# Column widths of the token tiles: 512 and 384 for 448 and 448 in the last layer but one, and 384 first in the early tiles

## The chip, the cores and the metric

The kernel runs on one core of one Trainium2 chip. The metric is the device time of one execution in microseconds (us); lower is better. TensorE is called PE below, VectorE DVE, ScalarE ACT, GpSimd POOL, and SyncE, which issues the loads, SP.

## The reference

```python
def _attn_ref(q, k, v):                      # 2 batches, 12 heads, 448 tokens, head size 64
    scores = np.matmul(q, k.transpose(0, 1, 3, 2)) / np.sqrt(64)
    scores = np.where(causal_mask, -1e9, scores)
    attn = softmax(scores)
    return np.matmul(attn, v)

def _moe_ref(x, w_in, w_out, alpha):         # 896 tokens, 768 -> 2048 -> 768
    h = x @ w_in
    g = np.maximum(h, 0.0) + alpha * np.minimum(h, 0.0)
    return g @ w_out

def _moe2_ref(x, w1, w2, w3, w_out):         # 896 tokens, 768 -> 768 -> 768
    h = np.maximum(np.maximum(x @ w1, x @ w2), x @ w3)
    return h @ w_out

# out = _moe2_ref(_moe_ref(attention as 896 x 768, ...), ...)
```

So there are four products by weight matrices after the attention: w_in (layer 1), w_out (layer 2), the three of w1, w2, w3 with a maximum over them (layer 3, the last but one), and the last w_out (layer 4).

## The kernel before, in words

**Precision.** Weights and activations are float32 values, each split into a high and a low part of the type fp32r. A product of two split values takes three matmuls (`product`, called on line 459): high by high, high by low, low by high. A weight matrix arrives as 64-bit words. The class `Weights` loads 128 output columns of it, converts the words on ACT (lines 422, 440) and DVE (lines 426, 429, 443, 454) and splits the result into `wh` (ACT, line 314) and `wl` (DVE, line 326). Four pairs `wh`, `wl` exist (ring `w`); the conversion runs ahead of PE by as many as are free.

**Tokens.** The activations lie transposed: 128 features in the partitions, the 896 tokens (2 batches of 448) in the free dimension. A PSUM bank holds 512 float32 columns, so the 896 tokens take two tiles, each with its own bank. Layers 1 and 2 use 512 and 384 columns (`CUT`, tokens 0 to 511 and 512 to 895, in layer 1; `LATE`, tokens 0 to 383 and 384 to 895, in layer 2). Layer 3 uses 448 and 448 (`HALF`). Layer 4 uses 448 columns throughout, because it computes its result by a scheme with seven products in place of eight over halves of the tokens and of the features; only its very last product is cut into 256 and 192 columns.

**Early tiles.** The first three blocks of 128 outputs of layer 1 (f = 0, 1, 2) begin while the last heads of the attention still run. Their first token tile is `SEQ[0]`, the 448 tokens of batch 0, in pieces of three matmuls (one of six feature blocks each) that are put into gaps of PE; their second tile is `SEQ[1]`, the 448 tokens of batch 1, after the attention. Each is followed by `prelu` on DVE and ACT. The slot of `w` that such a weight pair holds comes free with its second tile.

**Layer 3.** For each of six blocks f of 128 outputs, and each of w1, w2, w3, two products are made, one for each token tile, in an order that goes to and fro (`to_and_fro`: 1, 0, 0, 1, 1, 0, ...). One product is 6 feature blocks by 3 matmuls, 18 matmuls. The first result of a tile is copied out of its bank (ACT or DVE); the second and third are combined with the copy by a maximum on DVE (`larger`, line 984). Then the maxima are split (`h1`, `h2`, lines 314 and 326) and block sums of them are made for layer 4 (`room["t"]`, line 953). In the first three blocks the tile of batch 0 takes a buffer of the ring `mx` (three buffers of 448 columns), and that of batch 1 lies in the block sum's own place:

```python
m["m"] = room["t"][2][:, f] if kept else room["mx"].tile([P, S], F32, ...)
```

**Layer 4.** A step `third` waits for all products of layer 3; after it the operands of layer 4 are written over the tile that layer 3 read (`right`, `left`: casts and subtractions on ACT and DVE), while PE begins with the operands that are there already.

**Order.** Every engine executes its instructions in program order. That order comes from a list scheduler in the kernel's own code (`Plan`): each step has a rank, its cost on each engine that may do it, the steps it follows and the buffers it takes and gives; the step that can start first goes next, and of those within 0.02 us the one of the lowest rank. The cost of one matmul of n columns was `n / 2400 + 0.0134` us.

Of the kernel before, what the change touches and what calls it, by code (L numbers as in the profile page):

```python
# [25 lines left out]
NB = 3  # L26
# [36 lines left out]

def on_pool(n, two=True):
    return {"POOL": 0.18 + n * 2.1e-3 if two else 0.24 + n * 0.833e-3}


def on_dma(kb):
# [130 lines left out]
def attention_moe_moe2_kernel(  # L199
# [261 lines left out]
    class Product:  # L461


        def __init__(self, rank, pieces, bank, token, ranks=None):

            ranks = ranks or [rank] * len(pieces)
            total = len(pieces)
            self.end = None
            for i, (count, n, terms, after, give) in enumerate(pieces):
                self.end = plan.add(  # L470
                    ranks[i],
                    {"PE": count * 3 * (n / 2400 + 0.0134)},
                    step(self.issue, terms, bank, i == 0, i == total - 1),
                    list(after) + ([self.end] if self.end else []),
                    take=(token,) if i == 0 else (),
                    give=give,
                )
                if i == 0:
                    self.took = self.end
# [260 lines left out]
            return xT[i][:, self.hp, S * self.b : S * self.b + S]  # L740


    SEQ = tuple(slice(S * u, S * u + S) for u in range(B))
    CUT = tuple(slice(t, min(t + BANK, NT)) for t in range(0, NT, BANK))

    def to_and_fro(i, cut):
# [88 lines left out]
    for f, w in enumerate(held):  # L835
        r = FILL_RANK + FILL_STEP * f
        pieces = [
            (
                1,
                S,  # L840
                terms(w, lambda: xT, i, SEQ[0]),
                w.ready + [jobs[i].done],
                (("w", w.took),) * (i == KC - 1 and f < NB - HELD),
            )
            for i in range(KC)
        ]
        prod = Product(r, pieces, bank, "b")
        prelu(r + RANK["prelu"], prod, SEQ[0], f, lambda: early_g, "b")

# [13 lines left out]
    )  # L865
    for f in [*range(NB - HELD, NB), *(f for f in order if not NB - HELD <= f < NB)]:
        w = held[f] if NB - HELD <= f < NB else Weights(rank, w_in, 0, KC, f)
        us = SEQ[1:] if f < NB else [t for _, t in to_and_fro(f, CUT)]
        for u in us:
            after = w.ready + [j.done for j in jobs]  # L870
            pieces = [
                (
                    KC,
                    size(u),
                    lambda w=w, u=u: [t for i in range(KC) for t in terms(w, lambda: xT, i, u)()],
                    after,
                    (("w", w.took),) * (u == us[-1]),
                )
            ]
            prod = Product(rank, pieces, bank, "b")  # L880
            prelu(rank, prod, u, f, lambda: room["late_g"], "b")
        rank += 1
# [7 lines left out]
                self.it = self.make()  # L890
            return self.it

    LATE = (slice(0, NT - BANK), slice(NT - BANK, NT))
    yT = Lazy(lambda: pair(act, "x", [P, KC, NT]))
    y_done = {}
    for e in range(KC):
        pieces = [[] for _ in range(B)]
        for k, (k0, KW) in enumerate(((0, 6), (6, 5), (11, 5))):
            w = Weights(rank, w_out, k0, KW, e)
            for u, t in enumerate(LATE):  # L900
                pieces[u].append(
                    (
                        KW,
                        size(t),
                        lambda w=w, t=t, k0=k0, KW=KW: [
                            ([p[:, i, :] for p in w.parts], [p[:, t] for p in g[k0 + i]])
                            for i in range(KW)
                        ],
                        w.ready + [d for i in range(KW) for d in g_done[k0 + i]],
                        (("w", w.took),) * (u == (B - 1 if (e + k) % 2 == 0 else 0)),  # L910
                    )
                )
        prods = []
        for u in range(B):
            ranks = [rank + 0.2 * k + 0.1 * (u if (e + k) % 2 == 0 else 1 - u) for k in range(3)]
            prods.append(Product(rank, pieces[u], bank, "b", ranks))
        for u, t in enumerate(LATE):
            N = size(t)
            src = lambda u=u, N=N, prods=prods: prods[u].ps[:, :N]
            dst = lambda i, e=e, t=t: yT()[i][:, e, t]  # L920
            h = plan.add(rank, on_act(N, psum=True), copy(lambda dst=dst: dst(0), src), (prods[u].end,))
            y_done[u, e] = plan.add(
                rank,
                on_dve(N, psum=True),
                sub(lambda dst=dst: dst(1), src, lambda dst=dst: dst(0)),
                (h,),
                give=(("b", prods[u].took),),
            )
# [7 lines left out]
    def after_prelu():  # L936
# [1 line left out]
        early.close()  # L938
        last = ctx.enter_context(tc.tile_pool(name="last", bufs=1))
        room["tk"] = last  # L940
        room["mx"] = ctx.enter_context(tc.tile_pool(name="mx", bufs=3))
        room["h1"] = pair(last, "h1", [P, KH, S])
        room["h2"] = pair(last, "h2", [P, KH, NT])
        room["w1"] = pair(last, "w1", [P, KG, EH * P])
        room["w2"] = pair(last, "w2", [P, KH, EH * P])
        room["t"] = [last.tile([P, KH, S], F32, tag=f"t{i}", name=f"t{i}") for i in range(3)]
        room["s"] = [last.tile([P, KH, EH * P], F32, tag=f"s{i}", name=f"s{i}") for i in range(3)]
        plan.buffers(at=plan.end[second], mx=3, tk=1)

    second = plan.add(0, {"NONE": 0.0}, step(after_prelu), list(y_done.values()))  # L950
    def plus(out, a, b, op=ALU.add):
# [8 lines left out]
    h_done, t_done, s_done, products, low_done = {}, {}, {}, [], {}  # L960
    for f in range(KG):
        ws = [Weights(rank, w, 0, KC, f) for w in (w1, w2, w3)]
        m, m_end = [{} for _ in range(B)], [None] * B
        for i in range(3):
            for u, cut in to_and_fro(KG + f + i + 1, HALF):
                pieces = [
                    (
                        KC,
                        S,
                        lambda w=ws[i], u=cut: [t for x in range(KC) for t in terms(w, yT, x, u)()],  # L970
                        ws[i].ready + [y_done[v, e] for v in ((0, 1), (1,))[u] for e in range(KC)],
                        (("w", ws[i].took),) * (u == (B - 1 if (KG + f + i) % 2 else 0)),
                    )
                ]
                prod = Product(rank, pieces, bank, "b")
                products.append(prod.end)
                kept = f < KH and u == 1

                def first(m=m[u], f=f, kept=kept):
                    m["m"] = room["t"][2][:, f] if kept else room["mx"].tile([P, S], F32, tag="m", name="m")  # L980
                    return m["m"]

                def larger(prod=prod, m=m[u]):
                    nc.vector.tensor_tensor(
                        out=m["m"], in0=prod.ps[:, :S], in1=m["m"], op=ALU.max
                    )

                if i == 0:
                    m_end[u] = m_took = plan.add(
                        rank,  # L990
                        on_act(S, psum=True) | on_dve(S, psum=True),
                        copy(first, lambda prod=prod: prod.ps[:, :S]),
                        (prod.end,),
                        take=() if kept else ("mx",),
                        give=(("b", prod.took),),
                    )
                    m[u]["took"] = m_took
                else:
                    m_end[u] = plan.add(
                        rank,  # L1000
                        on_dve(S, psum=True),
                        step(larger),
                        (prod.end, m_end[u]),
                        give=(("b", prod.took),),
                    )
        k = f % KH
        for u in range(B):
            if f < KH and u == 1:
                continue
            dst = lambda i, f=f, k=k, u=u: room["h1"][i][:, k] if f < KH else room["h2"][i][:, k, HALF[u]]  # L1010
            src = lambda m=m[u]: m["m"]
            h = plan.add(rank, on_act(S), copy(lambda dst=dst: dst(0), src), (m_end[u],))
            h_done[u, f] = plan.add(
                rank,
                on_dve(S),
                sub(lambda dst=dst: dst(1), src, lambda dst=dst: dst(0)),
                (h,),
                give=(("mx", m[u]["took"]),) if f >= KH and u == 0 else (),
            )
        t = lambda i, k=k: room["t"][i][:, k]  # L1020
        m0, m1 = (lambda m=m[u]: m["m"] for u in range(B))
        if f < KH:
            t_done[0, k] = plan.add(
                rank,
                on_dve(S),
                step(plus(partial(t, 0), partial(t, 2), m0, ALU.subtract)),
                (m_end[1], h_done[0, f]),
                give=(("mx", m[0]["took"]),),
            )
        else:  # L1030
            t_done[1, k] = plan.add(
                rank,
                on_dve(S),
                step(plus(partial(t, 1), m1, partial(t, 0), ALU.subtract)),
                (m_end[1], t_done[0, k]),
            )
            t_done[2, k] = plan.add(
                rank,
                on_dve(S),
                step(plus(partial(t, 2), m1, partial(t, 2), ALU.subtract)),  # L1040
                (t_done[1, k], h_done[1, f]),
                give=(("mx", m[1]["took"]),),
            )
        r = f // 2
        c = slice(r * P, r * P + P)
# [155 lines left out]
    class Bank:  # L1201
# [3 lines left out]
        def add(self, rank, w, x, w_after, x_after, give=(), after=(), parts=(slice(0, S),)):  # L1205
            ends = []
            for cols in parts:
# [1 line left out]
                first = self.took is None  # L1209
                end = plan.add(  # L1210
                    rank,
                    {"PE": KH * 3 * (n / 2400 + 0.0134)},
                    step(self.issue, w, x, first, cols),
                    [*chain, *w_after, *x_after, *after],
                    take=("b",) if first else (),
# [254 lines left out]
```

## Time and profile before

| | |
|---|---|
| median of 3 runs | 492.85 us (491.95 to 492.85) |
| the profiled execution | 492.2 us |
| its span, first to last instruction | 490.4 us |
| granted clock of TensorE | 1.00 of full speed |
| busy: PE, DVE, ACT, POOL | 483.9, 384.6, 251.1, 51.8 us |

The span is what the trace covers; 1.8 us of the profiled execution's time lie outside it. Matmuls are pipelined: the time from one matmul's start to the next one's start is what PE needs for it, and is shorter than the duration that a row gives for it.

### The profile page before, as it was taken

What the parts mean: (1) busy time and instruction counts of PE and PEld (TensorE: products, weight loads), DVE (VectorE), ACT (ScalarE), POOL (GpSimd) and SP (SyncE); (2) the same over time, 40 slices, a digit from 0 to 9 for tenths busy, and PEclk for the clock granted to TensorE, in tenths of its full rate; (3) what the DMA queues carried; (4) which work ended last, traced back from release to release, by engine and by line L of the source; (5) the groups of instructions that cost most, each with busy time, mean ns of one, the idle gap of its engine ahead of it and who ended that gap; (6) DMA issues with size and microseconds to landing.
All of it is one profiled execution on the core that took longest, in us unless ns stands there. A gap on an engine that the chain in (4) does not pass through costs nothing.

```text
span 490.4 us, 7332 instructions
## 1 busy us (share of the span) xinstructions
PE 483.9 (99%) x2727; PEld 420.0 (86%) x2727; DVE 384.6 (78%) x751; ACT 251.1 (51%) x478; POOL 51.8 (11%) x100
## 2 busy tenths in 40 slices
PE   8999999999999999999999999999999999999997
PEld 4766768999988899889989989999999999999886
DVE  5789997589999999855756657599899998716962
ACT  6899995254455455432524434454564744305510
POOL 5657664000000000000000000000000000000000
PEclk9999999999999999999999999999999999999999
DMA  8666512113323343333334234344353633000122
GB/s 293 228 214 212 178 41 78 52 65 128 128 77 124 124 120 115 111 118 119 106 93 145 63 110 144 112 155 169 128 193 117 205 129 130 0 1 1 57 95 75
DMA packets 13859, 58.28 MB, mean 119 GB/s; under 512 B 1664, under 2 KB 3328, under 8 KB 13824
## 3 DMA queue, kind: packets, MB, share of 16 engines
q1 hardware_dynamic: 13680, 57.72, 35.2%
q8 instruction: 21, 0.34, 0.3%
q14 instruction: 14, 0.11, 0.1%
q10 hardware_dynamic: 144, 0.10, 0.1%
HBM read 55.06 MB, written 2.75 MB: 118 GB/s over the span
## 4 chain that ended last, share of the span: by engine, by line
PE 91%; ACT 5%; DVE 2%; issue 1%; POOL 0%; DVEq 0%; ACTq 0%
PE ps L459 82%; ACT e L672 3%; PE ps L641 3%; PE pv L731 3%; PE pt L716 3%; DVE e L659 1%; ACT p L314 1%; PE warm L797 1%; PE pt L713 0%; ACT xh L314 0%; ACT wh L314 0%; POOL e L689 0%; DVE wl L326 0%; DVE sm L684 0%; ACT r L440 0%
## 5 line engine op out<-in xcount | busy, mean ns | idle before, releaser
L459 PE MATMUL ps<-xh,wh 128*128 128x448 f32 (+2 forms) x435 | 159.4, 366 | 0.0
L459 PE MATMUL ps<-xh,wl 128*128 128x448 f32 (+2 forms) x435 | 159.2, 366 | 0.0
L459 PE MATMUL ps<-xl,wh 128*128 128x448 f32 (+2 forms) x435 | 159.1, 366 | 0.0
L459 PEld LDWEIGHTS ps<-xl,wh 128*128 128x128 f32 x435 | 81.7, 188 | 8.3
L459 PEld LDWEIGHTS ps<-xh,wl 128*128 128x128 f32 x435 | 81.6, 188 | 8.3
L459 PEld LDWEIGHTS ps<-xh,wh 128*128 128x128 f32 x435 | 81.7, 188 | 8.2
L314 ACT CAST wh<-t 128x768 fp32r<-128x768 f32 (+1 forms) x52 | 42.2, 812 | 63.3 <-DVE t L454 62.4
L459 PE MATMUL ps<-g_h,wl 128*128 128x384 f32 (+1 forms) x192 | 69.7, 363 | 0.0
L459 PE MATMUL ps<-g_l,wh 128*128 128x384 f32 (+1 forms) x192 | 69.6, 363 | 0.0
L459 PE MATMUL ps<-g_h,wh 128*128 128x384 f32 (+1 forms) x192 | 69.5, 362 | 0.0
L326 DVE TENSOR_TENSOR wl<-t,wh 128x768 fp32r<-128x768 f32 (+1 forms) x49 | 45.2, 922 | 18.0 <-ACT wh L314 18.0
L422 ACT ACTIVATE t<-raw 128x768 f32<-128x768 f32 (+1 forms) x58 | 51.2, 886 | 8.9 <-DMA raw<-in_moe_w_out_dram 2.9
L454 DVE CUSTOM_DVE_ANT_0 t<-t,r 128x1536 uint16<-128x1536 uint16 (+1 forms) x58 | 53.4, 925 | 2.1
L443 DVE SCALAR_TENSOR_TENSOR t<-raw,t 128x768 uint32<-128x768 uint32 (+1 forms) x58 | 53.7, 925 | 0.9
L440 ACT ACTIVATE r<-raw 128x768 uint32<-128x768 uint32 (+1 forms) x58 | 51.1, 881 | 3.9 <-DMA raw<-in_moe_w_in_dram 2.0
L689 POOL TENSOR_SCALAR e<-e,sm 128x192 f32<-128x192 f32 (+3 forms) x84 | 43.7, 539 | 29.8 <-DVE sm L685 18.7
L672 ACT ACTIVATE e<-e,nm 128x192 f32<-128x192 f32 (+3 forms) x84 | 43.9, 529 | 5.1 <-DVE nm L659 5.0
L314 ACT CAST g_h<-g 128x384 fp32r<-128x384 f32 (+2 forms) x32 | 18.1, 567 | 47.1 <-DVE g L769 47.0
L459 PEld LDWEIGHTS ps<-g_l,wh 128*128 128x128 f32 x192 | 36.0, 188 | 4.0
L459 PEld LDWEIGHTS ps<-g_h,wh 128*128 128x128 f32 x192 | 36.1, 188 | 3.9
L459 PEld LDWEIGHTS ps<-g_h,wl 128*128 128x128 f32 x192 | 36.0, 188 | 3.8
L659 DVE CUSTOM_DVE_ANT_0 e<-ps,mask 128x192 f32<-128x192 f32 (+2 forms) x72 | 32.1, 486 | 8.2 <-PE ps L641 7.9
(95 smaller groups left out, 521.9 us busy)
## 6 DMA issues: line engine op xcount, KB each, us to landing
raw<-in_moe_w_dram SPq DMA_DIRECT2D x18, 768.0 KB, 4.3
raw<-in_moe_w_in_dram SPq DMA_DIRECT2D x16, 768.0 KB, 4.4
raw<-in_moe_w_out_dram SPq DMA_DIRECT2D x12, 768.0 KB, 4.3
raw<-in_moe_w_out_dram SPq DMA_DIRECT2D x12, 640.0 KB, 4.1
qk<-in_qk_dram SPq DMA_DIRECT2D x12, 448.0 KB, 3.4
v<-in_v_dram SPq DMA_DIRECT2D x12, 448.0 KB, 4.8
out_dram<-o SPq DMA_DIRECT2D x11, 224.0 KB, 1.9
out_dram<-o SPq DMA_DIRECT2D x1, 128.0 KB, 1.7
```

The lines of the kernel that those rows point to most:

```text
L314: nc.scalar.copy(out(), src())
L326: ENGINE[engine].tensor_tensor(out=out(), in0=a(), in1=f32(b()), op=ALU.subtract)
L422: nc.scalar.activation(out=f32(self.t), in_=f32(self.raw[..., 1]), func=AF.Abs)
L440: nc.scalar.activation(out=self.r, in_=self.raw[..., 0], func=AF.Copy, scale=2.0**-29)
L443: nc.vector.scalar_tensor_tensor(out=self.t, in0=self.raw[..., 1], scalar=0xC0000000, in1=self.t, op0=ALU.bitwise_and, op1=ALU.bitwise_or,)
L454: ENGINE[engine].tensor_tensor(out=t, in0=t, in1=self.r.bitcast(I32), op=ALU.add)
L459: nc.tensor.matmul(ps, a, c, start=(first and y == 0), stop=(last and y == 2), **kw)
L641: nc.tensor.matmul(ps if c else ps[rows * j : rows * j + rows], self.qk[d, 0, START[c] : START[c] + rows], self.qk[d, 1, S - n :] if j els ...
L659: nc.vector.tensor_tensor_reduce(out=self.e_part(c, j), in0=self.ps[c, j], in1=masks[j][:, m : m + n] if c else short, op0=ALU.add, op1=AL ...
L672: nc.scalar.activation(out=s, in_=s, func=AF.Exp, scale=-1.0, bias=self.column(self.nm, i, c, j), accum_out=self.column(self.sm, i, c, j),)
L689: ENGINE[engine].tensor_scalar(out=s, in0=s, scalar1=self.column(self.sm, i, c, j), scalar2=1.0, op0=ALU.mult, op1=ALU.mult,)
L716: nc.tensor.transpose(pt[:, o : o + P], self.e[:, s : s + P], ident)
```

## The change

The token tiles of layers 1, 2 and 3 now all use `CUT`, 512 and 384 columns. In layer 2 that exchanges the two tiles' places (before, the first one was the narrow one). In layer 3 the products, first copies and maxima have 512 and 384 columns in place of 448 and 448. Because layer 4 still wants halves of 448, the maxima of both tiles go into one tile of 896 columns (`m["m"]`), whose halves the splits and block sums read; a split or sum that needs tokens 448 to 895 now waits for both tiles' maxima. In the first three blocks that tile is `both`, which holds the block sums 0 and 2 later; sum 0 is made in place. In the last three blocks it is one of two buffers of the ring `mx`. The early tiles take tokens 0 to 383 first (`EARLY`), which need batch 0 alone as before, and tokens 384 to 895 after the attention. The planner's cost of a matmul whose width is no multiple of 128 is 0.0066 us higher than before (`moved`).

```diff
+def moved(n):
+    return n / 2400 + (0.02 if n % 128 else 0.0134)
...
-                    {"PE": count * 3 * (n / 2400 + 0.0134)},
+                    {"PE": count * 3 * moved(n)},
...
-    SEQ = tuple(slice(S * u, S * u + S) for u in range(B))
+    EARLY = slice(0, NT - BANK)
...
-                S,
-                terms(w, lambda: xT, i, SEQ[0]),
+                size(EARLY),
+                terms(w, lambda: xT, i, EARLY),
...
-        prelu(r + RANK["prelu"], prod, SEQ[0], f, lambda: early_g, "b")
+        prelu(r + RANK["prelu"], prod, EARLY, f, lambda: early_g, "b")
...
-        us = SEQ[1:] if f < NB else [t for _, t in to_and_fro(f, CUT)]
+        us = [slice(EARLY.stop, NT)] if f < NB else [t for _, t in to_and_fro(f, CUT)]
...
-    LATE = (slice(0, NT - BANK), slice(NT - BANK, NT))
...
-            for u, t in enumerate(LATE):
+            for u, t in enumerate(CUT):
...
-        room["mx"] = ctx.enter_context(tc.tile_pool(name="mx", bufs=3))
+        room["mx"] = ctx.enter_context(tc.tile_pool(name="mx", bufs=2))
...
-        room["t"] = [last.tile([P, KH, S], F32, tag=f"t{i}", name=f"t{i}") for i in range(3)]
+        both = last.tile([P, KH, NT], F32, tag="t0", name="t0")
+        room["m"] = both
+        room["t"] = [both[:, :, HALF[0]], last.tile([P, KH, S], F32, tag="t1", name="t1"), both[:, :, HALF[1]]]
...
-            for u, cut in to_and_fro(KG + f + i + 1, HALF):
+            for u, cut in to_and_fro(KG + f + i + 1, CUT):
+                N = size(cut)
...
-                        ws[i].ready + [y_done[v, e] for v in ((0, 1), (1,))[u] for e in range(KC)],
+                        ws[i].ready + [y_done[u, e] for e in range(KC)],
...
-                def first(m=m[u], f=f, kept=kept):
-                    m["m"] = room["t"][2][:, f] if kept else room["mx"].tile([P, S], F32, tag="m", name="m")
-                    return m["m"]
-
-                def larger(prod=prod, m=m[u]):
+                def first(m=m, f=f, cut=cut):
+                    if not m:
+                        m["m"] = room["m"][:, f] if f < KH else room["mx"].tile([P, NT], F32, tag="m", name="m")
+                    return m["m"][:, cut]
+
+                def larger(prod=prod, m=m, N=N, cut=cut):
                     nc.vector.tensor_tensor(
-                        out=m["m"], in0=prod.ps[:, :S], in1=m["m"], op=ALU.max
+                        out=m["m"][:, cut], in0=prod.ps[:, :N], in1=m["m"][:, cut], op=ALU.max
                     )
...
-                        on_dve(S, psum=True),
+                        on_dve(N, psum=True),
...
-            src = lambda m=m[u]: m["m"]
-            h = plan.add(rank, on_act(S), copy(lambda dst=dst: dst(0), src), (m_end[u],))
+            src = lambda m=m, u=u: m["m"][:, HALF[u]]
+            h = plan.add(
+                rank, on_act(S), copy(lambda dst=dst: dst(0), src), m_end if u else m_end[:1]
+            )
...
-                step(plus(partial(t, 0), partial(t, 2), m0, ALU.subtract)),
-                (m_end[1], h_done[0, f]),
-                give=(("mx", m[0]["took"]),),
+                step(plus(partial(t, 0), partial(t, 2), partial(t, 0), ALU.subtract)),
+                (*m_end, h_done[0, f]),
...
-                    {"PE": KH * 3 * (n / 2400 + 0.0134)},
+                    {"PE": KH * 3 * moved(n)},
```

## Rows read from the trace of the kernel before

**Rows 1.** The page: the span, and the busy time of each engine.

```profile
span 490.4 us, 7332 instructions
PE 483.9 (99%) x2727; PEld 420.0 (86%) x2727; DVE 384.6 (78%) x751; ACT 251.1 (51%) x478; POOL 51.8 (11%) x100
```

**Rows 2.** The chain that ended last: start us, us, what.

```profile
85.62 376.32 PE ps L459 x1850
...
465.40 0.62 DVE o L1362
...
466.16 20.91 PE ps L459 x108
```

**Rows 3.** Windows: us, busy PE, PEld, DVE, ACT, POOL, clock, DMA share, GB/s.

```profile
85.62:103.28 17.66, 17.66 (x87) 16.38 (x88) 11.46 (x19) 6.07 (x10) 0.00 (x0) 1.00 0.10 40
103.28:197.35 94.07, 94.07 (x469) 84.66 (x468) 93.04 (x148) 47.78 (x68) 0.00 (x0) 1.00 0.35 115
197.35:313.18 115.83, 115.83 (x578) 104.24 (x576) 73.63 (x104) 47.16 (x66) 0.00 (x0) 1.00 0.35 112
313.18:447.09 133.91, 133.91 (x649) 121.64 (x649) 107.40 (x158) 62.35 (x84) 0.00 (x0) 1.00 0.34 118
...
447.09:466.16 19.07, 18.76 (x92) 16.74 (x90) 18.48 (x36) 13.19 (x28) 0.00 (x0) 1.00 0.10 37
...
331.00:404.00 73.00, 73.00 (x355) 66.31 (x354) 68.12 (x102) 40.55 (x54) 0.00 (x0) 1.00 0.46 158
```

**Rows 4.** Timeline of PE: start us, duration us, then the instruction and its form.

```profile
75.28 0.45 PE L459 MATMUL ps<-xh,wh 128*128 128x448 f32 x1
...
92.34 0.37 PE L459 MATMUL ps<-xh,wh 128*128 128x448 f32 x1
...
103.28 0.33 PE L459 MATMUL ps<-xh,wh 128*128 128x384 f32 x1
...
106.43 0.39 PE L459 MATMUL ps<-xh,wh 128*128 128x512 f32 x1
...
110.55 0.39 PE L459 MATMUL ps<-xh,wh 128*128 128x512 f32 x1
...
114.63 0.33 PE L459 MATMUL ps<-xh,wh 128*128 128x384 f32 x1
...
120.90 0.39 PE L459 MATMUL ps<-xh,wh 128*128 128x512 f32 x1
...
310.55 0.33 PE L459 MATMUL ps<-g_h,wh 128*128 128x384 f32 x1
...
313.18 0.36 PE L459 MATMUL ps<-xh,wh 128*128 128x448 f32 x1
...
395.01 0.37 PE L459 MATMUL ps<-xh,wh 128*128 128x448 f32 x1
...
447.09 0.37 PE L459 MATMUL ps<-h1h,w1h 128*128 128x448 f32 x1
```

**Rows 5.** Line 459 on PE in layer 3: duration min/median/max, first and last start.

```profile
L459 PE MATMUL ps<-xh,wh x216: 362/368/368, 313.2 to 446.5; 128*128 128x448 f32 x108
```

**Rows 6.** Groups by line and form: busy us, mean ns, idle before.

```profile
L984 DVE TENSOR_TENSOR m<-ps,m 128x448 f32<-128x448 f32 x18 | 11.2, 624 | 17.6 <-PE ps L459 17.3
...
L326 DVE TENSOR_TENSOR xl<-ps,xh 128x512 fp32r<-128x512 f32 x6 | 4.2, 692 | 14.6 <-ACT xh L314 14.6
...
L326 DVE TENSOR_TENSOR xl<-ps,xh 128x384 fp32r<-128x384 f32 x6 | 3.3, 557 | 9.8 <-ACT xh L314 9.8
```

**Rows 7.** Timeline of DVE, at four places.

```profile
108.17 0.95 DVE L326 TENSOR_TENSOR wl<-t,wh 128x768 fp32r<-128x768 f32 x1
...
311.37 0.69 DVE L326 TENSOR_TENSOR xl<-ps,xh 128x512 fp32r<-128x512 f32 x1 [3.46 <-ACT xh L314]
...
389.54 1.95 DVE L326 TENSOR_TENSOR wl<-t,wh 128x768 fp32r<-128x768 f32 x2
...
447.29 0.62 DVE L984 TENSOR_TENSOR m<-ps,m 128x448 f32<-128x448 f32 x1 [1.84 <-PE ps L459]
```

More of the change, by code (lines that the diff above doesn't have):

```diff
@@ L916, in attention_moe_moe2_kernel @@
             prods.append(Product(rank, pieces[u], bank, "b", ranks))
-        for u, t in enumerate(LATE):
+        for u, t in enumerate(CUT):
             N = size(t)
@@ L945, in after_prelu @@
         room["w2"] = pair(last, "w2", [P, KH, EH * P])
-        room["t"] = [last.tile([P, KH, S], F32, tag=f"t{i}", name=f"t{i}") for i in range(3)]
+        both = last.tile([P, KH, NT], F32, tag="t0", name="t0")
+        room["m"] = both
+        room["t"] = [both[:, :, HALF[0]], last.tile([P, KH, S], F32, tag="t1", name="t1"), both[:, :, HALF[1]]]
         room["s"] = [last.tile([P, KH, EH * P], F32, tag=f"s{i}", name=f"s{i}") for i in range(3)]
-        plan.buffers(at=plan.end[second], mx=3, tk=1)
+        plan.buffers(at=plan.end[second], mx=2, tk=1)
     second = plan.add(0, {"NONE": 0.0}, step(after_prelu), list(y_done.values()))
@@ L962, in attention_moe_moe2_kernel @@
         ws = [Weights(rank, w, 0, KC, f) for w in (w1, w2, w3)]
-        m, m_end = [{} for _ in range(B)], [None] * B
+        m, m_end, took = {}, [None] * B, None
         for i in range(3):
-            for u, cut in to_and_fro(KG + f + i + 1, HALF):
+            for u, cut in to_and_fro(KG + f + i + 1, CUT):
+                N = size(cut)
                 pieces = [
@@ L968, in attention_moe_moe2_kernel @@
                         KC,
-                        S,
+                        N,
                         lambda w=ws[i], u=cut: [t for x in range(KC) for t in terms(w, yT, x, u)()],
-                        ws[i].ready + [y_done[v, e] for v in ((0, 1), (1,))[u] for e in range(KC)],
+                        ws[i].ready + [y_done[u, e] for e in range(KC)],
                         (("w", ws[i].took),) * (u == (B - 1 if (KG + f + i) % 2 else 0)),
@@ L976, in attention_moe_moe2_kernel @@
                 products.append(prod.end)
-                kept = f < KH and u == 1
-                def first(m=m[u], f=f, kept=kept):
-                    m["m"] = room["t"][2][:, f] if kept else room["mx"].tile([P, S], F32, tag="m", name="m")
-                    return m["m"]
-                def larger(prod=prod, m=m[u]):
+                def first(m=m, f=f, cut=cut):
[3 more added lines that the diff above has]
+                def larger(prod=prod, m=m, N=N, cut=cut):
                     nc.vector.tensor_tensor(
-                        out=m["m"], in0=prod.ps[:, :S], in1=m["m"], op=ALU.max
+                        out=m["m"][:, cut], in0=prod.ps[:, :N], in1=m["m"][:, cut], op=ALU.max
                     )
                 if i == 0:
-                    m_end[u] = m_took = plan.add(
+                    m_end[u] = plan.add(
                         rank,
[L991 to L994, printed above, removed]
+                        on_act(N, psum=True) | on_dve(N, psum=True),
+                        copy(first, lambda prod=prod, N=N: prod.ps[:, :N]),
+                        (prod.end,) + ((took,) if took else ()),
+                        take=("mx",) * (f >= KH and took is None),
                         give=(("b", prod.took),),
                     )
-                    m[u]["took"] = m_took
+                    took = took or m_end[u]
                 else:
@@ L1017, in attention_moe_moe2_kernel @@
                 (h,),
-                give=(("mx", m[u]["took"]),) if f >= KH and u == 0 else (),
             )
         t = lambda i, k=k: room["t"][i][:, k]
-        m0, m1 = (lambda m=m[u]: m["m"] for u in range(B))
+        m0, m1 = (lambda m=m, u=u: m["m"][:, HALF[u]] for u in range(B))
         if f < KH:
@@ L1034, in attention_moe_moe2_kernel @@
                 step(plus(partial(t, 1), m1, partial(t, 0), ALU.subtract)),
-                (m_end[1], t_done[0, k]),
+                (*m_end, t_done[0, k]),
             )
@@ L1040, in attention_moe_moe2_kernel @@
                 step(plus(partial(t, 2), m1, partial(t, 2), ALU.subtract)),
-                (t_done[1, k], h_done[1, f]),
-                give=(("mx", m[1]["took"]),),
+                (t_done[1, k], h_done[0, f], h_done[1, f]),
+                give=(("mx", took),),
             )
```

## The prediction, made before the change was run

> **What bounds the kernel now.** I read the page first: PE is busy 483.9 of a span of 490.4 us, DVE 384.6 [rows 1]. Busy shares alone don't make a bound, so the chain that ended last comes next. From 85.62 us on it is one piece of 376.32 us of line 459 [rows 2]: through layers 1, 2, 3 and the start of layer 4, PE waits for nothing that the trace shows. After that one wait of PE remains, at 466.16, for a DVE instruction that ran from 465.40 to 466.02 [rows 2]. The windows by stage say the same: PE is busy for the whole of each stretch from 85.62 to 447.09, at a granted clock of 1.00, the level of 2.4 GHz [rows 3]. So what counts is how long PE takes from one matmul's start to the next, and any microsecond saved there comes off the end, as long as weights and free banks still arrive in time.
>
> **The price of a width.** The timeline gives it where the width changes [rows 4]. From 106.43 to 114.63 there are 36 matmuls of 512 columns: 8.20 / 36 = 227.8 ns each. From 114.63 to 120.90 there are 36 of 384: 6.27 / 36 = 174.2 ns. A pair covers 896 columns in 14.47 / 36 = 401.9 ns. Whole layers agree: layer 1 from 103.28 to 197.35 is 234 pairs (13 blocks of 18; the window's count has one matmul of the neighbour), 94.07 / 234 = 402.0 ns, and layer 2, 288 pairs, 115.83 / 288 = 402.2 ns [rows 3]. In these numbers the cost of changing from one width to the other, if there is one, is contained, and at the same frequency as in the new layer 3, about once in 36 matmuls. Layer 3 takes 133.91 us [rows 3] for 6 x 3 x 2 x 18 = 648 matmuls of 448: 206.7 ns each, 413.3 ns for the 896 columns. The early tiles show a third value: from 92.34 to 103.28 there are 54 of 448 [rows 4], 202.6 ns each.
>
> The same columns and the same number of instructions therefore cost 11.4 ns less as 512 + 384 than as 448 + 448 in layer 3, and 3.3 ns less than in the early tiles. From 384 to 512 a column costs 53.6 / 128 = 0.42 ns; at that slope a matmul of 448 would take 201.0 ns, so 448 carries an excess of 5.7 ns in layer 3 and 1.6 ns early on.
>
> The Trainium skill's page "TensorE: Matmul & The Clock Gate" (section "Back-to-back issue gap") speaks against this change: warm, it puts the gap at N / 2.4 ns plus a fixed 2.5 ns whatever N is. By it two matmuls cost 378.3 ns for 896 columns however they are cut, and layer 3 would gain nothing. The trace does not agree: its gaps are 227.8, 206.7 and 174.2 ns, where the page gives 215.8, 189.2 and 162.5, and the one of 448 lies off the line of the other two. I go by the rows and keep the rule's outcome as a rival.
>
> **The change, part by part.**
>
> Layer 3: 648 matmuls of 448 become 324 pairs. 324 x 401.9 = 130.2 us against 133.91: **-3.7 us**. With layer 2's 402.2 it would be -3.6; these bounds are close because each is a mean over hundreds.
>
> Early tiles: 54 pairs at 401.9 in place of 2 x 202.6 = 405.2 ns: **-0.2 us** in total. The first halves start at 75.28 [rows 4]; 21 of their 54 matmuls run before 85.62, between the steps of the last heads. Those 21 now take 21 x 28.4 ns = 0.6 us less. If the planner puts another piece there (3 matmuls, 0.52 us) nothing is lost; if PE idles instead, 0.6 us is lost. Bounds -0.2 to +0.4; I take -0.2, since pieces are left to fill with. The weights of the next block are the tightest of layer 1: their `wl` ends at 109.12 [rows 7] and PE wants them at 110.55 [rows 4]. The lead of 1.4 us stays nearly the same, as PE's total up to there does.
>
> Layer 2: the same widths with places exchanged. 0.
>
> Order at the seam: layer 2 now ends with its tile of 512 and layer 3 starts with the 384 others, 18 x 174.2 ns = 3.1 us, before it reads the 512. How long such a tile takes to be ready: PE had ended one at 310.55 [rows 4] and its `xl` was done at 312.06 [rows 7], 1.5 us later. Hidden, with 1.6 us to spare.
>
> First copies and maxima: DVE takes 692 ns for 512 columns and 557 for 384 out of PSUM, 1249 together, against 2 x 624 = 1248 [rows 6]. 0. The splits and block sums keep their count and width. Waiting for both maxima delays a block's sums by at most one product, 18 x 0.23 = 4.1 us; behind them on DVE stand conversions, see below. Two `mx` buffers: a block's buffer is wanted again two blocks later, and a block lasts 133.91 / 6 = 22.3 us. 0.
>
> Layer 4: PE's work is unchanged. DVE is nearly full there (18.48 of 19.07 us [rows 3]) and begins with the last maximum at 447.29, just behind PE's end of layer 3 [rows 4, 7]; the operands it then writes lie over what layer 3 reads, so its work moves forward together with PE. The last maximum has 384 columns now: 0.07 us less, off PE's wait at 466.16. **-0.1 us**. The dearer 448 in the planner can exchange steps on DVE; an instruction of DVE more or less ahead of that wait is about 0.6 us [rows 6], so -0.5 (the wait is gone: PE's last matmul before it began at about 465.5) to +0.6, or twice that if it happens in two rounds.
>
> What covers all this is the conversion of weights on DVE: 68.12 of 73.00 us between 331 and 404 [rows 3]. The tightest pair is the twelfth of layer 3: the first of the two `wl` from 389.54 ends at about 390.5 [rows 7], PE begins on it at 395.01 [rows 4]. PE will be there 11 x 18 x 11.4 ns + 0.2 = 2.4 us earlier, so 2.1 of 4.5 us of lead remain if DVE does not get faster. No stall.
>
> Sum: 492.2 (the profiled execution's own time: span 490.4 and 1.8 around it) - 3.7 - 0.2 - 0.1 = 488.2 us. That execution is 0.65 us under the median of the runs, which lie from 491.95 to 492.85; for the time of a median I add about half of that: **488.6 us**.
>
> **The rivals.**
>
> (a) More than that, 0.10: the 448s of layer 4 run at the early 202.6 ns (180 of them, 0.7 us), or PE's wait there goes. 487.6. Against it: layer 3 began after a run of 384, too, and ran at 206.7 from start to end; the durations hardly vary [rows 5].
>
> (b) Part is given back, 0.10: DVE's order in layer 4 or an idle PE between the last heads costs 0.6 to 1.5 us. 489.8.
>
> (c) The excess belongs to the stage and not to the width. If only the part by which layer 3 exceeds the early tiles does (4.1 ns a matmul), a pair costs 410.1 there and 1.0 us is gained: about 491.3, chance 0.04. If all 5.7 ns do, a pair costs 413.3: no gain in layer 3, 492.3, chance 0.05. For it: the same width ran at two rates. Against it: 512 and 384 ran alike in layers 1 and 2 while DVE was busy 99% and 64%, and nothing in layer 3's steady durations looks like interference. The skill's rule above ends in the same place.
>
> (d) Slower, 0.05: the weights come late in layer 3. Maxima that now wait in DVE's queue for the wider product push conversions back. It begins to cost when DVE is over 2.1 us later at the twelfth pair than now, and makes the kernel slower beyond 2.1 + 4.0 = 6.1 us; DVE has 4.9 us of slack in that stretch. With 7 us, 493.5.
>
> **How the numbers follow.** The forecast, 488.6 with a range of its own from 487.9 to 489.3, has 0.66. A measurement of this kernel tells about 0.2%, 1 us, from no change. Faster by more: forecast, (a), (b) and the first half of (c), 0.90. Within: the second half of (c), 0.05. Slower: (d), 0.05. The range that holds 8 in 10 takes in (a) and (b) but neither (c) nor (d), and the unknown half microsecond between an execution and a median: 487.2 to 490.2.
>
> **What would show it.** In the trace after, layer 3's stretch should last about 130.2 us with 36 matmuls of 512 in 8.2 us and 36 of 384 in 6.3; PE should have no idle time from about 85 to layer 4; layer 4 should last what it does now, 43.3 us from the first `h1` matmul to the end of the span. The prediction is wrong if the gap of 512 or 384 in layer 3 is above that of layers 1 and 2, if PE waits for `wl` around layer 3's twelfth weights, or if PE's wait in layer 4 grows past 1 us.

## The result, and the profile after

The changed kernel takes 488.2 us in the median of four runs (487.7 to 488.75) against 492.55 for the kernel before: a ratio of 0.9914, with a 95% interval from 0.9896 to 0.9931. That is 4.35 us faster, 0.4 us below the forecast and inside its range. Measured a second time it took 488.34, a ratio of 0.9914 again [0.9899, 0.9928].

The page of the changed kernel, to be set beside [rows 1] (line 463 of it is line 459 of the kernel before, 318 is 314, 330 is 326, 990 is 984): the span is 3.8 us shorter, and PE's busy time falls by nearly as much, while DVE's hardly changes.

```profile
span 486.6 us, 7335 instructions
PE 480.6 (99%) x2727; PEld 415.6 (85%) x2727; DVE 384.0 (79%) x750; ACT 250.3 (51%) x478; POOL 53.7 (11%) x101
```

Windows of the changed kernel (columns as in [rows 3]): layer 1, layer 3, the stretch from 331 to 404, and layer 4 up to PE's one wait. PE is still busy without a break up to layer 4.

```profile
103.75:197.75 94.00, 94.00 (x469) 84.63 (x468) 93.48 (x147) 46.93 (x67) 1.84 (x1) 1.00 0.34 115
313.62:443.84 130.22, 130.22 (x649) 117.23 (x648) 105.70 (x157) 62.68 (x84) 0.00 (x0) 1.00 0.36 122
331.00:404.00 73.00, 73.00 (x365) 65.72 (x364) 69.34 (x106) 40.91 (x55) 0.00 (x0) 1.00 0.46 161
443.84:462.74 18.90, 18.76 (x91) 16.74 (x91) 18.70 (x37) 13.55 (x29) 0.00 (x0) 1.00 0.10 37
```

Layer 3 takes 130.22 us where it took 133.91. The timeline of PE shows it run by run, to be read as [rows 4]: 36 matmuls of 512 from 316.76 to 324.96, 8.20 us; 36 of 384 from 324.96 to 331.23, 6.27 us, exactly what layer 1 pays.

```profile
75.93 0.42 PE L463 MATMUL ps<-xh,wh 128*128 128x384 f32 x1
...
91.47 0.39 PE L463 MATMUL ps<-xh,wh 128*128 128x512 f32 x1
...
103.75 0.33 PE L463 MATMUL ps<-xh,wh 128*128 128x384 f32 x1
...
313.62 0.33 PE L463 MATMUL ps<-xh,wh 128*128 128x384 f32 x1
...
316.76 0.39 PE L463 MATMUL ps<-xh,wh 128*128 128x512 f32 x1
...
324.96 0.33 PE L463 MATMUL ps<-xh,wh 128*128 128x384 f32 x1
...
331.23 0.39 PE L463 MATMUL ps<-xh,wh 128*128 128x512 f32 x1
...
393.22 0.39 PE L463 MATMUL ps<-xh,wh 128*128 128x512 f32 x1
...
443.84 0.36 PE L463 MATMUL ps<-h1h,w1h 128*128 128x448 f32 x1
```

Where the 3.8 us of span came from, by stage: up to the first early matmul the changed kernel is 0.65 us later (75.93 against 75.28), though its instructions there are the same in the same order, so this belongs to the execution and not to the change (two more runs of kernels alike up to there have 75.04 and 75.90); from there to the first 384 of layer 1 it takes 27.82 us against 28.00, -0.18; from there to layer 3, 209.87 against 209.90, nothing; layer 3, -3.69; layer 4 and the end, 42.78 against 43.29, -0.51. The part in layer 4 is larger than the prediction's 0.1. The chain that ended last in the changed kernel, to be set beside [rows 2], shows two pieces of it:

```profile
86.23 357.79 PE ps L463 x1776
...
444.04 0.56 DVE m L990
...
462.09 0.52 ACT wh L318
...
462.74 20.56 PE ps L463 x108
```

PE's wait in layer 4 is now for a cast on ACT, not for a DVE sum, and the stretch up to it is 18.90 us, 0.17 shorter than before [rows 3]. The 108 matmuls behind it take 20.56 us where they took 20.91 [rows 2], although they are the same matmuls: 0.35 us that no part of the change explains. It, and the early tiles' third price for 448 columns, led to the experiments.

### The profile page after: what moved, and what is told of

The parts are those of the page before. It is cut to its first block, busy times and chain, and to the rows that moved or that the text cites. A ratio compares the mean times of both kernels' runs of the same rounds, so it can differ in the third digit from the quotient of the medians.

```text
span 486.6 us, 7335 instructions
## 1 busy us (share of the span) xinstructions
PE 480.6 (99%) x2727; PEld 415.6 (85%) x2727; DVE 384.0 (79%) x750; ACT 250.3 (51%) x478; POOL 53.7 (11%) x101
## 4 chain that ended last, share of the span: by engine, by line
PE 88%; DVE 6%; ACT 5%; issue 1%; POOL 0%; DVEq 0%; ACTq 0%
PE ps L463 79%; PE ps L645 3%; ACT e L676 3%; PE pv L735 3%; PE pt L720 3%; DVE xl L330 1%; DVE e L663 1%; ACT p L318 1%; PE warm L801 1%; DVE wl L330 1%; DVE t L958 1%; PE pt L717 0%; ACT xh L318 0%; DVE v L1141 0%; ACT wh L318 0%
## 5 line engine op out<-in xcount | busy, mean ns | idle before, releaser
L463 PE MATMUL ps<-xh,wl 128*128 128x384 f32 (+2 forms) x435 | 158.0, 363 | 0.0
L463 PE MATMUL ps<-xh,wh 128*128 128x384 f32 (+2 forms) x435 | 157.9, 363 | 0.0
L463 PE MATMUL ps<-xl,wh 128*128 128x384 f32 (+2 forms) x435 | 157.8, 363 | 0.0
L463 PE MATMUL ps<-g_h,wl 128*128 128x512 f32 (+1 forms) x192 | 69.7, 363 | 0.0
L463 PE MATMUL ps<-g_l,wh 128*128 128x512 f32 (+1 forms) x192 | 69.6, 363 | 0.0
L463 PE MATMUL ps<-g_h,wh 128*128 128x512 f32 (+1 forms) x192 | 69.5, 362 | 0.0
L330 DVE TENSOR_TENSOR wl<-t,wh 128x768 fp32r<-128x768 f32 (+1 forms) x48 | 44.2, 921 | 17.6 <-ACT wh L318 17.6
L318 ACT CAST g_h<-g 128x384 fp32r<-128x384 f32 (+1 forms) x32 | 18.2, 568 | 49.4 <-DVE g L773 49.3
```

The source lines that it names most:

```text
L318: nc.scalar.copy(out(), src())
L330: ENGINE[engine].tensor_tensor(out=out(), in0=a(), in1=f32(b()), op=ALU.subtract)
L463: nc.tensor.matmul(ps, a, c, start=(first and y == 0), stop=(last and y == 2), **kw)
```

## The experiments

The prediction put layer 3's gain on the width, and kept "the excess belongs to the stage" as a rival. It had seen that 448 columns cost 202.6 ns in the early tiles and 206.7 in layer 3, and had no reason for it. The experiments first take the change apart, and then look for that reason.

**The early tiles alone, and without them.**

```diff
# the changed kernel with the early tiles of before
-    EARLY = slice(0, NT - BANK)
+    EARLY = slice(0, S)
# the kernel before with the early tiles of the changed one
+    EARLY = slice(0, NT - BANK)
...
-                S,
-                terms(w, lambda: xT, i, SEQ[0]),
+                size(EARLY),
+                terms(w, lambda: xT, i, EARLY),
...
-        us = SEQ[1:] if f < NB else ...
+        us = [slice(EARLY.stop, NT)] if f < NB else ...
```

> The changed kernel, but its early tiles take 448 and 448 columns again. Width theory (a 448 costs 202.6 ns early on, a 384 and a 512 together 401.9): the stretch from the first early matmul to the first 384 of layer 1 goes back from 27.8 to 28.0 us, layer 3 stays at 130.2 us, the time rises by 0.2 us to about 488.4. Rival (idle PE between the last heads decides what the early tiles are worth): the stretch changes by 0.5 us or more in either direction, or PE shows idle time before 86 us.

> The kernel before with nothing changed but the early tiles, 384 columns first and 512 after. Width theory: the early stretch 27.8 us against 28.0, layer 3 unchanged at 133.9 us, 492.3 us, which can't be told from before by time. Rival: the early tiles carry a good part of the 4.3 us between the two kernels, 491 us or less.

Measured: 488.79 us, ratio 0.9922 [0.9907, 0.9936], for the changed kernel with 448 first; 492.19 us, 0.9991 [0.9981, 1.0000], for the early part alone. The timeline of PE in the latter gives the stretch from the first early matmul to layer 1's first 384:

```profile
75.13 0.42 PE L459 MATMUL ps<-xh,wh 128*128 128x384 f32 x1
...
102.94 0.33 PE L459 MATMUL ps<-xh,wh 128*128 128x384 f32 x1
```

27.81 us, where the kernel before has 28.00; in the changed kernel with 448 first it is 28.01 (75.04 to 103.05), where the changed kernel has 27.82. So the early tiles are worth 0.2 us, as predicted, and layer 3 of the former still takes 130.2 us: they carry none of the rest. The time of the former, 0.4 us over what was expected, doesn't tell: its four runs lie from 487.7 to 489.0.

**The planner's cost.** Two runs, one with the old cost in the changed kernel and one with the new cost in the kernel before.

```diff
# changed kernel, old cost
-    return n / 2400 + (0.02 if n % 128 else 0.0134)
+    return n / 2400 + 0.0134
# kernel before, new cost (here and at one more place)
-                    {"PE": count * 3 * (n / 2400 + 0.0134)},
+                    {"PE": count * 3 * moved(n)},
```

> The changed kernel with the planner's old cost of a matmul, 0.0134 us beside its columns whatever its width; only the order of DVE and ACT in layer 4 differs from the changed kernel. If the new cost is what removed PE's wait in layer 4: the wait of about 0.5 us is back, layer 4 takes 43.3 us in place of 42.8, 488.7 us. Rival (the shorter last maximum, or nothing but chance in the order, removed it): layer 4 stays at 42.8 us.

> The kernel before with nothing changed but the planner's cost of a matmul of 448 columns. If the new cost alone orders layer 4 better: layer 4 takes 42.8 us in place of 43.3 and the time is 492.0. Layer 3 should still take 133.9 us, its matmuls being the same. Rival: layer 4 stays at 43.3 us or gets longer, and the time is 492.5 or more.

Measured: 488.29 us, 0.9918 [0.9901, 0.9934], and 492.06 us, 0.9993 [0.9984, 1.0003]. PE's wait is the time between the last matmul of one operand and the first of the next, less one gap of 0.2 us. First the changed kernel with the old cost, then the kernel before with the new one:

```profile
462.28 0.37 PE L463 MATMUL ps<-xh,w2l 128*128 128x448 f32 x1
...
462.67 0.44 PE L463 MATMUL ps<-h2h,wh 128*128 128x448 f32 x1
```

```profile
465.86 0.37 PE L463 MATMUL ps<-xh,w2l 128*128 128x448 f32 x1
...
466.43 0.44 PE L463 MATMUL ps<-h2h,wh 128*128 128x448 f32 x1 [0.21 <-ACT wh L318]
```

The waits are 0.2 and 0.4 us; they were 0.5 in the kernel before (465.49 to 466.16, less a gap) and 0.3 in the changed one (462.23 to 462.74). The old cost did not bring the wait back, so the new cost is not what shortened it in the changed kernel. In the kernel before, the numbers expected of the new cost did come out, 492.06 us and 42.84 us from the first `h1` matmul to the end in place of 43.29, but for the most part by luck: only 0.1 us of it is the wait; the rest is the last 108 matmuls, which took 20.56 us here as well (466.43 to 486.99), and a repetition of the changed kernel below shows that this differs between executions of one program. Each of these four orders of DVE and ACT has a wait of its own between 0.2 and 0.5 us, and none can be told from another by time.

**One tile for the maxima, without any width.** The changed kernel with the widths and costs of before.

```diff
+    LATE = (slice(0, NT - BANK), slice(NT - BANK, NT))     # layer 2 as before; EARLY = slice(0, S)
-            for u, cut in to_and_fro(KG + f + i + 1, CUT):
+            for u, cut in to_and_fro(KG + f + i + 1, HALF):
```

> The changed kernel with every width and cost of the kernel before (448 and 448 in layer 3 and in the early tiles, layer 2 with 384 first), so that only the maxima in one tile and the two buffers of 896 columns are left of the change. If these cost nothing: layer 3 at 133.9 us, entered from 384 and so at 206.7 ns a matmul, no idle PE in it, and 492.4 us. If waiting for both tiles' maxima pushes the conversions back: PE idle time in layer 3 and more than 493 us.

Measured: 492.12 us, 0.9992 [0.9982, 1.0002]; the window of layer 3:

```profile
313.71:447.62 133.91, 133.91 (x649) 121.62 (x649) 107.14 (x158) 62.24 (x84) 0.00 (x0) 1.00 0.35 118
```

133.91 us, to the hundredth what it was [rows 3], with no idle PE. The tile and its waits cost nothing.

**Other widths, and 448 everywhere.**

```diff
# changed kernel, another cut in each block of layer 3
+        edge = (512, 480, 448, 464, 496, 456)[f]
+        cuts = (slice(0, edge), slice(edge, NT))
-            for u, cut in to_and_fro(KG + f + i + 1, CUT):
+            for u, cut in to_and_fro(KG + f + i + 1, cuts):
...
# kernel before, 448 and 448 in layers 1 and 2
-        us = ... [t for _, t in to_and_fro(f, CUT)]
+        us = ... [t for _, t in to_and_fro(f, SEQ)]
-    LATE = (slice(0, NT - BANK), slice(NT - BANK, NT))
+    LATE = SEQ
```

> The changed kernel with another cut in each of layer 3's six blocks: 512 and 384, 480 and 416, 448 and 448, 464 and 432, 496 and 400, 456 and 440 columns. If a matmul costs a fixed part and its columns (0.42 ns each), with 448 alone an exception, every other pair costs 402 ns. If what counts is whether 128 divides the width, as the planner's cost has it: 402 for the first, 413 for all others. If it is 64: as before, with 448 cheap, which the trace before excludes. If it is 32: 480 and 416 cost 402, 464 and 432, 496 and 400, 456 and 440 cost 413. The block of 448 and 448 stands between other widths here: 413 if the width sets the rate, 405 if it depends on what ran before.

> The kernel before with 448 and 448 columns in layers 1 and 2 as well, so that no width changes before layer 4's end. If the width alone sets the time of a matmul at 206.7 ns: layer 1 takes 234 pairs x 413.3 ns = 96.7 us (94.1 before), layer 2 119.0 us (115.8), and the kernel 498.3 us. If the stage sets it and the early rate of 202.6 ns holds in layers 1 and 2: 94.8 and 116.7 us, 494 us, and layer 3 keeps 133.9. If the rate of 202.6 is a state that lasts until a width changes: layer 3 too falls to 648 x 202.6 ns = 131.3 us and the kernel takes about 491.

The first took 489.25 us in one run. The timeline of PE in its layer 3, where the width changes:

```profile
345.96 0.38 PE L463 MATMUL ps<-xh,wh 128*128 128x480 f32 x1
...
353.77 0.35 PE L463 MATMUL ps<-xh,wh 128*128 128x416 f32 x1
...
357.13 0.37 PE L463 MATMUL ps<-xh,wh 128*128 128x448 f32 x1
...
379.02 0.37 PE L463 MATMUL ps<-xh,wh 128*128 128x464 f32 x1
...
382.78 0.36 PE L463 MATMUL ps<-xh,wh 128*128 128x432 f32 x1
...
389.84 0.37 PE L463 MATMUL ps<-xh,wh 128*128 128x464 f32 x1
...
397.39 0.36 PE L463 MATMUL ps<-xh,wh 128*128 128x432 f32 x1
...
400.87 0.34 PE L463 MATMUL ps<-xh,wh 128*128 128x400 f32 x1
...
404.17 0.38 PE L463 MATMUL ps<-xh,wh 128*128 128x496 f32 x1
...
412.09 0.34 PE L463 MATMUL ps<-xh,wh 128*128 128x400 f32 x1
...
418.69 0.38 PE L463 MATMUL ps<-xh,wh 128*128 128x496 f32 x1
...
426.38 0.36 PE L463 MATMUL ps<-xh,wh 128*128 128x440 f32 x1
...
433.57 0.37 PE L463 MATMUL ps<-xh,wh 128*128 128x456 f32 x1
...
441.06 0.36 PE L463 MATMUL ps<-xh,wh 128*128 128x440 f32 x1
```

Runs of 36: 480 columns in 7.81 us (216.9 ns each), 432 in 7.06 (196.1), 464 in 7.55 (209.7), 496 in 7.92 (220.0), 400 in 6.60 (183.3), 440 in 7.19 (199.7), 456 in 7.49 (208.1); 416 in a run of 18, 3.36 us (186.7). The pairs cost 403.6 (480 and 416), 403.3 (496 and 400), 405.8 (464 and 432) and 407.8 ns (456 and 440): none is near 413, so neither 128 nor 32 columns make a rule. The first theory falls too: not every pair costs 402, and 448 is no exception, for the straight line through 384 and 512 gives 204.3 ns for 456 columns, which took 208.1. Nor is 448 the only width with two values: 18 matmuls of 432, from 397.39 to 400.87, took 193.3 ns each, against 196.1 in the run of 36. The block of 448 and 448, 108 matmuls from 357.13 to 379.02, takes 202.7 ns each, in the very stage where it took 206.7 before.

With 448 everywhere the kernel takes 491.3 us, 0.9977 [0.9967, 0.9986]: not slower, as the width theory had it, but 1.1 us faster than before. Its layer 3 lasts 131.3 us, 202.7 ns a matmul, with nothing in layer 3 changed:

```profile
314.97:446.29 131.32, 131.32 (x649) 121.86 (x648) 106.19 (x156) 62.81 (x85) 0.00 (x0) 1.00 0.35 121
```

So 448 columns have two rates at the same granted clock, the stage does not choose between them, and the one that the early tiles start with lasted for some 1,870 matmuls until PE's wait in layer 4.

**What chooses the rate.** In the kernel before, what ran ahead of layer 3 was a run of 384; ahead of the block in the run of widths, 416. The entry theory, as the expectations call it, is that the run ahead of a stretch of 448 sets its rate, and that the rate then lasts for the stretch. Call 202.7 ns the short gap and 206.7 the long one. The next two kernels put breaks into the kernel with 448 everywhere.

```diff
-        us = ... [t for _, t in to_and_fro(f, SEQ)]
+        us = ... [t for _, t in to_and_fro(f, CUT if f in (5, 10) else SEQ)]          # two breaks
+        us = ... [t for _, t in to_and_fro(f, CUT if f in (4, 7, 10, 13) else SEQ)]   # four breaks
```

> The kernel with 448 and 448 in every layer, but with blocks 5 and 10 of layer 1 cut 512 and 384. Block 5 runs 384 first and 512 last, block 10 512 first and 384 last. Entry theory: 202.6 ns up to block 5; after 512 one rate or the other; after block 10, whose last run has 384 columns, 206.7 ns from there to the end of layer 4, 133.9 us in layer 3. If the rate belongs to runs of 448 that are long, it stays at 202.6 throughout.

> The kernel with 448 and 448 in every layer, but with blocks 4, 7, 10 and 13 of layer 1 cut 512 and 384. Blocks 4 and 10 end with 384 columns, blocks 7 and 13 with 512. Entry theory, as the run with two breaks has it: 206.7 ns in blocks 5 and 6, 202.6 in 8 and 9, 206.7 in 11 and 12, 202.6 from block 14 through layers 2 and 3 (layer 3 at 131.3 us) up to PE's wait in layer 4. If the first run of 384 sets the rate for good, or the rate after a break is chance: 206.7 to the end, or another sequence.

Two breaks: 497.48 us in one run, 6.2 us more than with none. After 512 the 144 matmuls from 125.82 to 155.01 take 202.7 ns; after the 384 that ends at 162.26 every 448 takes 206.7 until layer 4, 133.9 us in layer 3. Four breaks: 492.01 us in one run, and the sequence that was expected. Its timeline of PE:

```profile
118.49 0.36 PE L459 MATMUL ps<-xh,wh 128*128 128x448 f32 x1
...
133.36 0.34 PE L459 MATMUL ps<-xh,wh 128*128 128x384 f32 x1
...
140.61 0.36 PE L459 MATMUL ps<-xh,wh 128*128 128x448 f32 x1
...
155.20 0.39 PE L459 MATMUL ps<-xh,wh 128*128 128x512 f32 x1
...
162.44 0.36 PE L459 MATMUL ps<-xh,wh 128*128 128x448 f32 x1
...
177.32 0.34 PE L459 MATMUL ps<-xh,wh 128*128 128x384 f32 x1
...
184.56 0.36 PE L459 MATMUL ps<-xh,wh 128*128 128x448 f32 x1
...
447.22 0.37 PE L459 MATMUL ps<-h1h,w1h 128*128 128x448 f32 x1
```

The 72 matmuls of 448 behind 384 take 14.87 and 14.88 us (118.49 to 133.36, 162.44 to 177.32), the 72 behind 512 take 14.59 (140.61 to 155.20), and from 184.56, again behind 512, the short gap holds through layer 2 and layer 3 (315.89 to 447.22, 131.3 us).

**The kernel before, with layer 3 entered from another width.**

```diff
     for e in range(KC):
+        edge = 416 if e == KC - 1 else NT - BANK
+        LATE = (slice(0, edge), slice(edge, NT))
```

> The kernel before, layer 3 at 448 and 448 as it was; only the last of layer 2's six blocks is cut 416 and 480 in place of 384 and 512, so that the run ahead of layer 3's first matmul has 416 columns. Entry theory (448 runs at 202.6 or 206.7 ns according to what ran before it, and keeps that rate): layer 3 falls from 133.9 to 131.3 us with no change to it, layer 4's 180 matmuls of 448 save another 0.7, and the time is about 489.2. Width theory (448 beside other widths costs 206.7): 492.4, layer 3 at 133.9.

Measured: 489.92 us, 0.9945 [0.9928, 0.9961], 2.6 us below the 492.48 of the kernel before that was measured with it. The window of its layer 3, line 459 on PE in it (to be set beside [rows 5]), and the wait in layer 4:

```profile
313.82:445.15 131.33, 131.33 (x649) 121.73 (x648) 106.36 (x156) 62.77 (x85) 0.00 (x0) 1.00 0.35 121
```

```profile
L459 PE MATMUL ps<-xh,wh x216: 362/365/369, 313.8 to 444.5; 128*128 128x448 f32 x108
```

```profile
463.19 0.37 PE L459 MATMUL ps<-xh,w2l 128*128 128x448 f32 x1
...
463.93 0.44 PE L459 MATMUL ps<-h2h,wh 128*128 128x448 f32 x1 [0.37 <-DVE o L1364]
```

131.33 us for layer 3 with its widths untouched. The two rates can be told apart by the durations: the median is 365 ns here and 368 in [rows 5]. From 320 to 420 us all 483 matmuls recorded of the kernel before last 368 ns; of the 493 of this run 296 last 365 ns, 99 last 362 and 98 last 369. The expected 489.2 was not reached: of layer 4's 0.7 us, PE's wait took back 0.1 (0.5 us now, as it arrives earlier than DVE), and behind the wait the long gap was back.

**Layer 4 entered from 416.** This and the changed kernel were measured together.

```diff
# changed kernel
+        edge = 480 if f == KG - 1 else BANK
+        cuts = (slice(0, edge), slice(edge, NT))
-            for u, cut in to_and_fro(KG + f + i + 1, CUT):
+            for u, cut in to_and_fro(KG + f + i + 1, cuts):
...
```

> The changed kernel with the last of layer 3's six blocks cut 480 and 416, so that layer 4 is entered from 416 columns. Entry theory: the 162 matmuls of 448 ahead of the last products and the 18 after them take 202.6 ns in place of 206.7, 0.7 us less, against 54 x 1.6 = 0.1 us more in the block: 0.6 us under the changed kernel, about 487.7. Width theory: 0.1 us over the changed kernel.

> The changed kernel once more, on the same chip as the one with the last block cut 480 and 416, to be compared with it: 488.2 us, layer 3 at 130.2 us, its 448s of layer 4 at 206.7 ns.

Measured: 488.16 us, 0.9913 [0.9898, 0.9928], and 488.34 us, 0.9914 [0.9899, 0.9928] for the changed kernel: no difference. The first 90 matmuls of layer 4 do run at 202.7 ns (89 gaps, 18.04 us from 443.18 to 461.22), but then:

```profile
461.22 0.36 PE L463 MATMUL ps<-xh,w2l 128*128 128x448 f32 x1
...
462.12 0.44 PE L463 MATMUL ps<-h2h,wh 128*128 128x448 f32 x1 [0.54 <-ACT wh L318]
```

The wait is 0.7 us in place of 0.3. DVE and ACT set the end of this stretch, 18.94 us long here and 18.90 in the changed kernel; what PE gains in it becomes a wait. The chain of the changed kernel's repetition shows one thing more:

```profile
462.72 20.91 PE ps L463 x108
```

Here the same program as above took 20.91 us for its last 108 matmuls, and 20.56 there. After a wait, the rate of 448 differed from one execution to the next.

## Why the prediction was right, and where its reason was not

**The sum held.** Layer 3: predicted -3.7, measured -3.69. Early tiles: -0.2, measured -0.18, and -0.19 in each of the two runs that took them by themselves. Layers 1 and 2: 0, measured -0.03. One tile, maxima, two buffers: 0, and 0 in the run that had them alone. The sum needed no reason for the difference between its two prices: 206.7 ns for 448 was layer 3's own, and 401.9 for the pair came from layer 1, where the same widths alternate as in the new layer 3. DVE's maxima took what the splits of the same width showed:

```profile
L990 DVE TENSOR_TENSOR m<-ps,m 128x512 f32<-128x512 f32 x6 | 4.1, 690 | 8.3 <-PE ps L463 8.3
...
L990 DVE TENSOR_TENSOR m<-ps,m 128x384 f32<-128x384 f32 x6 | 3.3, 556 | 7.2 <-PE ps L463 7.2
```

**Layer 4** was put at -0.1 and measured at -0.51. Of that, 0.17 is a shorter wait, inside the bounds I gave, and 0.35 the short gap behind it, which the repetition of the same program did not have. Without that 0.35 the traces give the change 0.18 + 0.03 + 3.69 + 0.17 = 4.1 us, where the prediction's sum was 4.0. The 0.4 us added to the sum for a median did not show: the medians, 488.2 and 488.34, lie at the sum itself.

**The lead of the weights**, rival (d): PE begins on the twelfth pair of layer 3 at 393.22. DVE's timeline in the changed kernel:

```profile
389.07 0.95 DVE L330 TENSOR_TENSOR wl<-t,wh 128x768 fp32r<-128x768 f32 x1
```

It ends at 390.02, so 3.2 us of lead are left, where the prediction allowed 2.1; DVE became a little denser in that stretch, 69.34 of 73.00 us, and kept ahead.

**The reason was only half of it.** The step "448 carries an excess of 5.7 ns in layer 3" read a property of the width out of two rows with different values. The runs showed that the excess over the line is not 448's own, that 448 has two rates, 202.7 and 206.7 ns, and that the run of matmuls just before has a part in which of them comes: 384 gave the long gap (the kernel before, the changed kernel's layer 4, both runs with breaks), 512 and 416 the short one (both runs with breaks; three kernels entered from 416). Of the 11.4 ns that a pair saves in layer 3, 7.9 are the long gap, 324 x 7.9 = 2.6 us, which the kernel before also sheds when only the run ahead of layer 3 is changed; 3.5 ns, 1.1 us, are 512 and 384 against 448 and 448 at its better rate. The change holds one more way to the short gap, in a part that the prediction put at 0: it lets layer 2 end with 512 columns in place of 384. By the runs with breaks that alone would have given a layer 3 of 448 the short gap; no run shows it. Rival (c), the stage, is out: the same stage showed both rates. Rival (a) came half true in the first trace. The reason given against it held for the 90 matmuls ahead of PE's wait, which followed 384 and ran at the long gap as layer 3 had; that layer 3 kept its rate to the end said nothing of the 90 that come after a wait.

The Trainium skill's rule of the page "TensorE: Matmul & The Clock Gate" (section "Back-to-back issue gap"), a fixed 2.5 ns beside N / 2.4, is given there for an isolated matmul, which the prediction left out, and not for a stream of weight loads and matmuls such as this one. Taken for the stream, it would have left layer 3 at its old length. The trace after does not agree: 130.22 us against 133.91.

**What stays open.** Why 384 leads into the long gap and 512 into the short one, and what a wait does to it, is not settled. The runs show that it is so, in eleven entries into 448 from 384 and in six from 416 or 512, and not what carries it. In the run of widths layer 4 was entered from 440 and began with the long gap as well, so the rate does not simply rise or fall with the width. Nor does it take a change of width: of the fourteen traces, five show the short gap behind PE's wait in layer 4 and nine the long one, with 448 on both sides of it. Where the last matmul ahead of the wait began at least 0.67 us before the first one behind it, the long gap came, eight times of eight; where it was 0.39 to 0.57 us, the short one did, five times of six. The sixth is the repetition of the changed kernel: 0.51 us there, as in the first trace of that kernel, and the other gap. That the moment of entry decides, and the width only by way of it, is a rival that no run here tests.

## What to carry to other kernels

Where PE is the bound, read the time from start to start for each shape in each stage, and when one shape shows two values, look at what ran just before each before calling either of them its price: here most of a gain put down to tile widths was also to be had by changing one run of matmuls ahead of the stage. A pair of widths should be compared by its sum over the same columns, with the changes of width in it. And a gain on PE counts only as far as PE sets the end of the stretch: in layer 4, where DVE and ACT do, 0.4 us less on PE became 0.4 us of waiting.

## What the runs showed of the hardware that was not expected

At a granted clock of 1.00, the level of 2.4 GHz, matmuls of 448 fp32r columns followed one another every 202.7 or every 206.7 ns. Each rate lasted for as long as nothing but 448 came and PE did not wait, some 1,490 matmuls at the long one in one run and 1,870 at the short one in another, through different operands and layers. In the runs with breaks 18 matmuls of 384 columns led into the long gap three times of three, and 18 of 512 into the short one three times of three, two of these out of the long one. Behind a wait of PE, both gaps came, and both in executions of one program. For 896 columns, the cheapest pair was 512 and 384 with 401.9 ns; 448 and 448 cost 405.4 at the short gap and 413.3 at the long one, and the dearest of the other pairs was 456 and 440 with 407.8.
